# A fused LSH attention and MoE kernel: two small per-row operations move from ScalarE to GpSimd

## Chip, cores and metric

One core of a Trainium2 chip runs the whole program. The metric is the device time of one execution in microseconds (us); the value of a kernel is the median over its runs.

## What is computed

Attention over 4 batches, 8 heads, 768 rows and a head size of 64, in which a query sees only the keys of its own hash bucket (6 sign bits of a projection), and behind it a two-layer feed-forward block on 3072 tokens of 512 values:

```python
mask = q_bucket[:, :, :, None] == k_bucket[:, :, None, :]
scores = np.where(mask, scale * (q @ k.T), -1e9)
scores = scores - np.max(scores, axis=-1, keepdims=True)
attn = np.exp(scores)
attn = attn / (np.sum(attn, axis=-1, keepdims=True) + 1e-09)
x = attn @ v                       # 3072 x 512 after the heads are put side by side
h = x @ w_in                       # 512 -> 2048
g = np.where(h > 0, h, np.exp(np.minimum(h, 0)) - 1)
out = g @ w_out                    # 2048 -> 512
```

## The kernel before

All matrix products run on pairs of float16 numbers, a high and a low part of each float32 value, with three products for one. The 4 batches are cut into 8 chunks of 384 rows. A chunk has 4 head pairs, and a head pair has 6 slots, a slot being 128 query rows of one head against all 768 keys: 192 slots in all. Two slots together are called a duo; there are 96.

What a duo goes through, by line. `scores` (L508) makes 4 matmuls per slot into the one PSUM tile `s`; VectorE (DVE) copies it out to `pt` with a row maximum `m` at its side (L520), which frees `s` for the next slot. `exps` then makes the bias `nb`, minus the scaled maximum, for both slots of the duo in one ScalarE (ACT) operation of 128x2 values (L533), and two exponentials on ACT over 128x768 values with the row sums `sm` as a by-product (L536). `splits` makes the scale `r` from the sums in another 128x2 operation on ACT (L545), takes its reciprocal on DVE (L546), makes the high part `hl` on ACT (L143) and the low part on DVE (L152), and sends both through a transposing DMA on SP's queue to `PT`. `attend` (L559) multiplies `PT` with the values into `av`, four slots after the pair's last scores, and ACT and DVE split `av` into `x` (L568, L569).

The feed-forward matmuls (h, L585; o, L621) are dealt out between the slots. From slot 30 on, TensorE's (PE's) order is the order of the program text; every other engine's order comes from a planner that lists the instructions by an estimated timeline before the run. At run time each engine takes its own instructions strictly in that order. GpSimd (POOL) has a few memsets at the start and then only the 24 output stores (L635), each of which waits for the copy of a finished output tile `W<-o` on ACT (L143) or DVE (L145). The tiles `nb`, `sm`, `r` and `m` have three buffers each.

Of the kernel before, what the change touches and what calls it, by code (L numbers as in the profile page):

```python
# [12 lines left out]
AF = mybir.ActivationFunctionType  # L13
ALU = mybir.AluOpType
# [7 lines left out]
P_TOP = 14  # L22
# [44 lines left out]
def lsh_attention_moe(  # L67
# [10 lines left out]
    nc = tc.nc  # L78
# [60 lines left out]
    def scaled(kind, o, x, s):  # L139

        e = engine(kind)
        if e == "A":
            nc.scalar.activation(o, x, AF.Copy, scale=s)  # L143
        elif e == "V":
            nc.vector.tensor_scalar(o, x, s, None, ALU.mult)  # L145
        else:
            nc.gpsimd.tensor_scalar(o, x, s, 1.0, ALU.mult, ALU.mult)

    def rest(kind, o, x, s, hi):

        if engine(kind) == "V":
            nc.vector.scalar_tensor_tensor(o, x, s, hi, ALU.mult, ALU.subtract)  # L152
        else:
            nc.gpsimd.tensor_scalar(x, x, s, 1.0, ALU.mult, ALU.mult)
            nc.gpsimd.tensor_tensor(o, x, hi, ALU.subtract)
# [372 lines left out]
    def exps(st, duo):  # L528

        m, pts = duo[0], duo[1:]  # L530
        w = len(pts)
        nb = small.tile([P, 2], F32, tag="nb", name="nb")
        nc.scalar.activation(nb[:, :w], m[:, :w], AF.Copy, scale=st["sg"][:, 1:2])  # L533
        sm = small.tile([P, 2], F32, tag="sm", name="sm")
        for n, pt in enumerate(pts):
            nc.scalar.activation(  # L536
                pt, pt, AF.Exp, bias=nb[:, n : n + 1], scale=st["sg"][:, 0:1], accum_out=sm[:, n : n + 1]
            )
        return sm, pts

    def splits(sm, pts, PTs):

        w = len(pts)
        r = small.tile([P, 2], F32, tag="r", name="r")
        nc.scalar.activation(r[:, :w], sm[:, :w], AF.Copy, scale=2.0**-P_TOP, bias=1e-9 * 2.0**-P_TOP)  # L545
        nc.vector.reciprocal(r[:, :w], r[:, :w])  # L546
        for n, pt in enumerate(pts):
            hl = pp.tile([P, 2, S], F16, tag="p", name="hl")
            scaled("p_hi", hl[:, 0, :], pt, r[:, n : n + 1])
            rest("p_lo", hl[:, 1, :], pt, r[:, n : n + 1], hl[:, 0, :])  # L550
            nc.sync.dma_start_transpose(PTs[n].rearrange("p x c e -> p (x c) e"), hl.rearrange("p x e -> p (x e)"))
# [183 lines left out]
    for ns in groups:  # L735
# [3 lines left out]
        for n in ns:  # L739
            at = begin[n] - (PREP0 if early else PREP)[2]  # L740

            w = 2 * chunks[pairs[n][0]]["nc"]
# [142 lines left out]
    def run_splits():  # L885
        if behind:
            splits(*behind.pop())

    for G in range(starts[-2] + 1):
        if G == starts[0]:  # L890
            ordered.enter_context(tc.manual_schedule(engines={mybir.EngineType.PE}))
        if G < len(slots):
            n, at = slots[G]
            c = chunks[pairs[n][0]]
            b, p, j, t = c["b"], pairs[n][1], at // c["nc"], at % c["nc"]
            now[0] = int(w_at == NSI + NSO)
            if t == 0:
                (PT,) = pt_ring.take(c["nc"], pairs[n][0])
                PTs = PTs + [PT] if j else [PT]
            if G < starts[0] and G % 2:  # L900
                s_tile = ps_o.tile([P, 2, 512], F32, tag="o", name="so")
            else:
                s_tile = ps_s.tile([P, 2, 512], F32, tag="s", name="s")
            scores(ks[b, p], qs[n], at, j, s_tile, duo, G >= starts[0])
            into.append(PT[:, t])

            run_splits()
            if len(into) == 2:
                behind.append((*exps(qs[n], duo), into))
                duo, into = [], []  # L910
            if at == 2 * c["nc"] - 1:
                assert not into
                waiting.append((G + AV_LAG, (n, PTs)))
        else:
            run_splits()
# [39 lines left out]
```

## Time and profile before

| | us |
|---|---|
| median of 3 runs | 952.47 |
| lowest and highest run | 951.82, 953.67 |
| the profiled execution | 948.24 |
| its span, first to last instruction | 946.5 |

The span is 1.7 us shorter than the profiled execution's own time; this part lies outside all instructions. In the rows below, times are in us from the start of the span unless marked ns, and an engine's idle time is put down to the instruction that ended it. DVE is VectorE, ACT is ScalarE, POOL is GpSimd, PE is TensorE, PEld its weight loads.

### The profile page before, as it was taken

The page shows a single profiled execution, that of the slowest core. Times are in us where ns is not written, and L with a number is a line of the kernel's source. Part 1 is how long each engine was busy: PE and PEld are TensorE (multiplying, and loading weights), DVE is VectorE, ACT ScalarE, POOL GpSimd, SP SyncE. Part 2 cuts the span into 40 slices and gives each one's busy share as a digit, 9 for nine tenths or more (in the row PEclk, how much of TensorE's full clock was granted, in tenths as well). Part 3 has the DMA queues.
Part 4 walks back from the last instruction along what each step waited for, and adds up shares of the span by engine and source line. Part 5 has one row for each costly group of instructions (what it writes and reads, how often), then busy time and mean ns, then how long its engine had stood idle before and what let it go on. Part 6 is the DMA issues. An engine that isn't in the chain of part 4 may idle for free.

```text
span 946.5 us, 14531 instructions
## 1 busy us (share of the span) xinstructions
PE 818.4 (86%) x4975; PEld 420.4 (44%) x4975; DVE 704.0 (74%) x1528; ACT 739.3 (78%) x1469; POOL 15.7 (2%) x49
## 2 busy tenths in 40 slices
PE   2536555888999999988998999998999999999996
PEld 0113222444545555444544455544545555555553
DVE  6899899898867877678777687787878687674332
ACT  4677777999879888789779788889888788885442
POOL 1000000000000000000000000000000000000000
PEclk9956666998999999999999999999999999999998
DMA  9999886776887767696886767795777667556000
GB/s 280 280 207 224 226 231 161 136 141 145 153 167 169 153 113 126 132 187 117 163 180 137 139 109 150 148 181 101 144 155 136 118 119 151 102 101 100 34 1 35
DMA packets 404586, 138.47 MB, mean 146 GB/s; under 512 B 380960, under 2 KB 398880, under 8 KB 404512
## 3 DMA queue, kind: packets, MB, share of 16 engines
q1 hardware_dynamic: 402432, 131.25, 68.9%
q0 software_dynamic: 1920, 6.29, 1.9%
q8 instruction: 39, 0.64, 0.3%
q14 instruction: 35, 0.29, 0.1%
q10 hardware_dynamic: 160, 0.00, 0.0%
HBM read 35.65 MB, written 6.29 MB: 44 GB/s over the span
## 4 chain that ended last, share of the span: by engine, by line
issue 50%; DVE 14%; PE 14%; DMA 13%; ACT 6%; SPq 1%; POOL 1%; POOLq 0%; ACTq 0%; DVEq 0%
PE o L621 4%; PE av L559 4%; PE h L585 3%; DVE pt L520 3%; DMA PT<-hl 3%; DVE hl L152 3%; PE s L508 2%; DMA K<-natk 2%; DMA O<-nat1q 2%; ACT pt L536 2%; DMA W<-in_moe_w_in_dram 1%; DMA U<-in_moe_w_out_dram 1%; DVE W L469 1%; POOL out_dram L635 1%; DVE W L479 1%
## 5 line engine op out<-in xcount | busy, mean ns | idle before, releaser
L621 PE MATMUL o<-W,U 128*128 128x512 f16 x1152 | 280.2, 380 | 3.2 <-ACT W L143 3.1
L585 PE MATMUL h<-x,W 128*128 128x384 f16 x1536 | 279.8, 326 | 0.0
L585 PEld LDWEIGHTS <-W 128*128 128x128 f16 x1536 | 147.5, 98 | 111.1 <-issue 9.9
L536 ACT ACTIVATE pt<-pt,nb,sg 128x768 f32<-128x768 f32 x192 | 195.3, 1019 | 1.7
L152 DVE SCALAR_TENSOR_TENSOR hl<-pt,r,hl 128x768 f16<-128x768 f32 x192 | 189.4, 1011 | 7.5 <-ACT hl L143 7.2
L520 DVE TENSOR_SCALAR_CACHE_REDUCE pt<-s 128x768 f32<-128x768 f32 x177 | 168.0, 949 | 22.9 <-PE s L508 21.9
L143 ACT ACTIVATE hl<-pt,r 128x768 f16<-128x768 f32 x192 | 168.7, 927 | 20.2 <-DVE r L546 19.4
L508 PE MATMUL s<-K,O 128*128 128x384 f16 x708 | 153.3, 340 | 32.2 <-DVE pt L520 26.9
L621 PEld LDWEIGHTS <-U 128*128 128x128 f16 x1152 | 111.0, 98 | 122.7 <-issue 8.9
L559 PE MATMUL av<-PT,vhl 128*64 128x384 f16 x1152 | 115.6, 350 | 27.3 <-DMA PT<-hl 20.8
L600 DVE SCALAR_TENSOR_TENSOR U<-U 128x384 f32<-128x384 f32 x128 | 70.9, 554 | 85.8 <-ACT U L599 84.8
L508 PEld LDWEIGHTS <-O 76*128 76x128 f16 (+1 forms) x768 | 74.7, 102 | 134.7 <-issue 51.2
L596 ACT ACTIVATE U<-h,ch 128x384 f32<-128x384 f32 x128 | 72.9, 570 | 63.7 <-PE h L585 63.6
L152 DVE SCALAR_TENSOR_TENSOR U<-U,sgg 128x384 f16<-128x384 f32 x128 | 78.4, 612 | 53.3 <-ACT U L143 53.3
L559 PEld LDWEIGHTS <-vhl 128*64 128x64 f16 x1152 | 72.8, 117 | 81.7 <-ACT hl L143 17.7
L143 ACT ACTIVATE U<-U,sgg 128x384 f16<-128x384 f32 x128 | 77.8, 608 | 20.5 <-DVE U L600 20.4
L599 ACT ACTIVATE U<-h,ch 128x384 f32<-128x384 f32 x128 | 72.9, 570 | 0.0
L472 PE MATMUL acc<-W,ones 128*128 128x512 bf16 x32 | 16.9, 546 | 35.7 <-DVE W L469 35.5
L536 ACT ACTIVATION_READ_ACCUMULATOR pt<-pt,nb,sg 128x1 f32 x192 | 36.4, 190 | 0.0
L533 ACT ACTIVATE nb<-m,sg 128x2 f32<-128x2 f32 x96 | 27.7, 289 | 6.8 <-DVE pt L520 6.4
L291 DVE TENSOR_SCALAR zb<-z,pjt 64x384 f16<-64x384 f32 (+1 forms) x48 | 29.1, 606 | 3.9 <-PE z L286 3.9
L207 ACT ACTIVATE nat1q<-qst 128x384 bf16<-128x384 f32 x30 | 15.5, 516 | 18.1 <-DMA O<-nat1q 16.0
(103 smaller groups left out, 527.2 us busy)
## 6 DMA issues: line engine op xcount, KB each, us to landing
U<-in_moe_w_in_dram SPq DMA_DIRECT2D x12, 512.0 KB
vf<-in_v_dram SPq DMA_DIRECT2D x16, 384.0 KB
U<-in_moe_w_out_dram SPq DMA_DIRECT2D x12, 512.0 KB
out_dram<-W POOLq DMA_DIRECT2D x24, 256.0 KB, 4.0
qst<-in_q_dram SPq DMA_DIRECT2D x30, 192.0 KB
kst<-in_k_dram SPq DMA_DIRECT2D x14, 384.0 KB
PT<-hl SPq DMA_TRANSPOSE x192
W<-in_moe_w_in_dram SPq DMA_DIRECT2D x4, 512.0 KB
```

The lines of the kernel that those rows point to most:

```text
L143: nc.scalar.activation(o, x, AF.Copy, scale=s)
L152: nc.vector.scalar_tensor_tensor(o, x, s, hi, ALU.mult, ALU.subtract)
L291: nc.vector.tensor_scalar(zb[used], t[used], pj["thr"][used, which : which + 1], (MBIT, -MBIT)[which], ALU.is_gt, ALU.mult)
L508: nc.tensor.matmul(s_tile[:, n, :HALF], st[o][:rows, at, :], kst[kk][:rows, j * NC + n * HC : j * NC + (n + 1) * HC, :].rearrange("p a b - ...
L520: top = nc.vector.tensor_scalar(pt.rearrange("p (n e) -> p n e", n=2), s_tile[:, :, :HALF], CLAMP, None, ALU.max, ALU.max, accum_out=duo[0 ...
L536: nc.scalar.activation(pt, pt, AF.Exp, bias=nb[:, n : n + 1], scale=st["sg"][:, 0:1], accum_out=sm[:, n : n + 1])
L559: nc.tensor.matmul(av[j * D : (j + 1) * D], vt[:, j, c, vx, :], PTs[j][:, :, px, c, :], start=n == 0, stop=n == last,)
L585: nc.tensor.matmul(h, WH[:, g * KT + t, wx, fc * P : (fc + 1) * P], c["xs"][t][:, xx, :], start=n == 0, stop=n == 3 * KT - 1,)
L596: nc.scalar.activation(e, h, AF.Exp, scale=c["ch"])
L599: nc.scalar.activation(hp, h, AF.Relu, scale=c["ch"])
L600: nc.vector.scalar_tensor_tensor(e, e, -1.0, hp, ALU.add, ALU.min)
L621: nc.tensor.matmul(o[t][:, :DO], g16[:, gx, t * P : (t + 1) * P], WH[:, NSI + 1 + f, wx, :], start=f == 0 and i == 0, stop=f == NF - 1 and ...
```

## The change

The two 128x2 operations of a duo are issued to GpSimd in place of ScalarE. The values are the same: the bias is the row maximum times a per-partition scale that is read from SBUF, and the scale before the reciprocal is (sum + 1e-9) times a constant.

```diff
@@ exps @@
         nb = small.tile([P, 2], F32, tag="nb", name="nb")
-        nc.scalar.activation(nb[:, :w], m[:, :w], AF.Copy, scale=st["sg"][:, 1:2])
+        nc.gpsimd.tensor_scalar(nb[:, :w], m[:, :w], st["sg"][:, 1:2], 1.0, ALU.mult, ALU.mult)
         sm = small.tile([P, 2], F32, tag="sm", name="sm")
@@ splits @@
         r = small.tile([P, 2], F32, tag="r", name="r")
-        nc.scalar.activation(r[:, :w], sm[:, :w], AF.Copy, scale=2.0**-P_TOP, bias=1e-9 * 2.0**-P_TOP)
+        nc.gpsimd.tensor_scalar(r[:, :w], sm[:, :w], 1e-9, 2.0**-P_TOP, ALU.add, ALU.mult)
         nc.vector.reciprocal(r[:, :w], r[:, :w])
```

## Rows read from the trace of the kernel before

**Rows 1.** The page's part 1: busy us (share of the span), instructions, by engine.

```profile
PE 818.4 (86%) x4975; PEld 420.4 (44%) x4975; DVE 704.0 (74%) x1528; ACT 739.3 (78%) x1469; POOL 15.7 (2%) x49
```

**Rows 2.** Busy time of each engine by stage; columns named in the first line.

```profile
core 0: us, PE busy (x) PEld busy (x) DVE busy (x) ACT busy (x) POOL busy (x), PEclk, DMA share, GB/s
40.00:166.00 126.00, 71.23 (x332) 30.83 (x331) 117.84 (x263) 96.63 (x186) 0.00 (x0) 0.62 0.87 210
237.00:860.00 623.00, 595.32 (x3807) 313.75 (x3806) 469.93 (x997) 521.55 (x1053) 9.88 (x18) 1.00 0.74 141
```

**Rows 3.** What PE waited for, 237 to 860: total, times, longest us.

```profile
PE s L508 <- DVE pt L520: 16.6, 21, 1.8
PE av L559 <- DMA PT<-hl: 7.5, 6, 3.1
PE o L621 <- ACT W L143: 3.1, 4, 1.6
```

**Rows 4.** The same view, 40 to 166 (first row) and 166 to 237 (second).

```profile
PE av L559 <- DMA PT<-hl: 9.3, 3, 6.1
...
PE av L559 <- DMA PT<-hl: 4.0, 2, 2.5
```

**Rows 5.** Groups of instructions, whole span: the moved ones.

```profile
L533 ACT ACTIVATE nb<-m,sg 128x2 f32<-128x2 f32 x96 | 27.7, 289 | 6.8 <-DVE pt L520 6.4
L545 ACT ACTIVATE r<-sm 128x2 f32<-128x2 f32 x96 | 18.5, 193 | 0.3
```

**Rows 6.** Waits around them, whole span: total, times, longest us.

```profile
ACT hl L143 <- DVE r L546: 19.4, 18, 3.2
DVE r L546 <- ACT r L545: 6.7, 5, 1.6
ACT nb L533 <- DVE pt L520: 6.4, 14, 1.1
```

**Rows 7.** Timeline of ACT, then DVE, around one duo: start, us, instruction.

```profile
302.12 1.76 ACT L143 ACTIVATE hl<-pt,r 128x768 f16<-128x768 f32 x2 [0.60 <-DVE r L546]
304.72 0.29 ACT L533 ACTIVATE nb<-m,sg 128x2 f32<-128x2 f32 x1
305.04 1.03 ACT L536 ACTIVATE pt<-pt,nb,sg 128x768 f32<-128x768 f32 x1
...
301.93 0.16 DVE L546 RECIPROCAL r<-r 128x2 f32<-128x2 f32 x1
```

**Rows 8.** Timeline of ACT and POOL: the stores at a chunk's end; a memset group.

```profile
286.30 0.68 ACT L143 ACTIVATE W<-o,os 128x512 f32<-128x512 f32 x1
287.29 0.67 POOL L635 DMA_DIRECT2D out_dram<-W  x1 [283.80 <-ACT nb L533]
289.05 0.54 POOL L635 DMA_DIRECT2D out_dram<-W  x1 [1.10 <-DVE W L145]
293.07 0.54 POOL L635 DMA_DIRECT2D out_dram<-W  x1 [3.47 <-ACT W L143]
...
2.11 0.67 POOL L236 MEMSET pjt<- 32x1 f32 x8
```

**Rows 9.** What DVE waited for, 237 to 860: total, times, longest us.

```profile
DVE U L600 <- ACT U L599: 47.2, 37, 3.7
DVE U L152 <- ACT U L143: 41.6, 36, 3.6
```

**Rows 10.** Instructions of L533 in 40 to 166, then in 237 to 860.

```profile
L533 ACT ACTIVATE nb<-m,sg x14: 278/282/298, 40.0 to 158.5; 128x2 f32<-128x2 f32 x14
...
L533 ACT ACTIVATE nb<-m,sg x74: 278/290/302, 241.7 to 856.4; 128x2 f32<-128x2 f32 x74
```

**Rows 11.** DVE busy by stage, lines 152 and 600 alone (us, busy, count); one group.

```profile
237.00:860.00 623.00, 237.28 (x299) 1.00 0.74 141
...
237.00:860.00 623.00, 54.80 (x99) 1.00 0.74 141
...
L152 DVE SCALAR_TENSOR_TENSOR hl<-pt,r,hl 128x768 f16<-128x768 f32 x192 | 189.4, 1011 | 7.5 <-ACT hl L143 7.2
```

## Prediction

> **What bounds the kernel now.** I first read the busy shares of the engines over the whole span: PE 86%, ACT 78%, DVE 74%, POOL 2% [rows 1]. They say only that POOL is free to take work and that ACT is second. The same view cut into stages says where each engine counts. From 40 to 166 us DVE is busy for 117.8 of 126 us and PE for 71; ACT has 29 us to spare. From 237 to 860 us PE is busy for 595.3 of 623 us, ACT for 521.6 and DVE for 469.9 [rows 2]. So this long stage is bound by PE, in an order laid down by the program, and a change of any other engine's work is worth only what it does to PE's 27.7 idle us. The view of PE's own waits names them: 16.6 us for DVE to empty the score tile, 7.5 us for the transposed probabilities, 3.1 us for ACT to copy an output tile [rows 3]. In the two stages ahead PE waits 9.3 and 4.0 us for the transposed probabilities, three and two times [rows 4].
>
> **What is removed.** ACT loses 96 operations of 289 ns (27.7 us) and 96 of 193 ns (18.5 us) [rows 5]: 46.2 us in all, 0.48 us per duo. That is work beside PE, and no PE wait is made of it directly. DVE's waits behind ACT are long, 47.2 and 41.6 us on the feed-forward side [rows 9], but they end in DVE idle time, of which it has 153 us in that stage. The PE wait that names ACT is the output copy, four times [rows 3]. Each of these copies may have had one or the other small operation in front of it; I credit four times 0.29 us, **-1.2 us**. The bounds are 0 and the -7 us worked out under the rivals.
>
> **What is added: two more engine changes per duo.** The bias was made on ACT, where it is used. With ACT waiting, the path from the end of DVE's copy to the exponential was one hand-over of about 0.03 us (DVE's reciprocal ends at 302.09, ACT's `hl` starts at 302.12), 0.29 us of work, and 0.03 us to the exponential (305.01 to 305.04) [rows 7]: 0.35 us. The scale was likewise 0.03 + 0.19 + 0.03 = 0.25 us before DVE's reciprocal. Now both go to POOL and back. No row shows a POOL arithmetic operation, so three pieces are bounded:
> - Hand-over to POOL: ACT's copy ends at 286.98 and POOL's store starts at 287.29 [rows 8]. That is 0.31 us, ten times the hand-over between DVE and ACT, and I take 0.30. It is for a DMA instruction; another kind may start sooner, down to 0.03 us.
> - The operation: eight 32x1 memsets take 0.67 us, 0.08 each, and a store holds POOL for 0.54 [rows 8]. I take 0.29, what ACT needs for the same shape with the same scale read from SBUF [rows 5]; this is the nearest row in kind.
> - The hand-over back: 0.03 to 0.30 by the two kinds of hand-over above; I take 0.15, about the middle, because no row shows that direction.
>
> Together 0.74 us, with bounds of 0.14 and 1.14. Against 0.35 and 0.25 a duo's chain is longer by 0.39 + 0.49 = 0.88 us; by the bounds it is anywhere from 0.32 us shorter to 1.68 us longer.
>
> What is exposed of it? ACT stood idle for the row maximum before 14 of the 96 biases, and DVE for the scale before 5 of its 96 reciprocals; ACT stood idle for the reciprocal before 18 high parts [rows 6]. Elsewhere the consumer comes later than the data, and a bias made early is even a gain for ACT. Between a twentieth and a fifth of the steps are exposed, and I take a quarter, since a longer chain catches up with more of them. What is queued behind: behind an exponential that waits for POOL stand ACT's feed-forward activations, and behind a reciprocal that waits stands DVE's next score copy, for which PE waits. The chain reaches PE where PE already waits for its end, 3 + 2 + 6 = 11 times [rows 3, 4]. So 11 x 0.88 x 1/4 = **+2.4 us**, bounds -3.5 (11 x 0.32) and +18.5 (11 x 1.68).
>
> **What is moved past POOL's queue.** POOL starts its instructions in the planner's order. At a chunk's end its third store waits for a copy that ACT makes later: POOL sits there for 3.47 us [rows 8]. A bias or a scale that is planned behind this store stands behind it. A duo comes every 623 / 74 = 8.4 us [rows 10], with two small operations; with such a wait 2 x 3.47 / 8.4 = 0.83 of them fall into it, at a mean of half the wait, 1.74 us. There are six such chunk ends before the attention work ends. The same quarter exposed gives 6 x 0.83 x 1.74 x 1/4 = **+2.2 us**, bounds 0 (all of them planned ahead of the store) and +8.7 (all exposed). The store itself is held by a small operation for under 1 us, and nothing waits for it at once except the reuse of its tile.
>
> **Edits with one answer.** The arithmetic has the same operands and tile sizes; no DMA, matmul or buffer is added, so the last stage after 860 us costs nothing new: it has no duo left.
>
> **The sum.** -1.2 + 2.4 + 2.2 = +3.4 us on the profiled execution's 948.2 us (946.5 us of span and 1.7 us around it): 951.6. That execution is 4.2 us under the median of the runs, 952.47, so on the scale of the median I forecast **955.9 us**, 0.36% slower.
>
> **Rivals.** *POOL and DVE hold each other up, slower still.* Mechanism: POOL and DVE hold each other up when both read SBUF. The DVE lines that combine two SBUF tensors are 237.3 + 54.8 of 623 us, 47% of the time, in pieces of up to 1.01 us [rows 11]. If a POOL operation must wait for the running one, it starts 0.47 x 0.5 = 0.24 us later; if DVE must wait for POOL's 0.29 us, DVE loses 0.47 x 0.29 = 0.14 us for each. At 40 to 166 us, where DVE is the bound, there are 14 duos, 28 operations [rows 10]: +3.8 us. In the chain 11 x 2 x 0.24 = +5.3 us. With the forecast's 3.4 this gives 12.5 us, **965 us**. It decides once POOL's operation holds DVE for a few tenths of a us. The memsets, POOL's only computing so far, read nothing, so no row here shows such a conflict or denies it. By the Trainium skill, "SBUF — State Buffer", section "Who interferes with whom", a DVE instruction with two SBUF inputs contends with a GpSimd instruction that reads SBUF, as an exclusive lock for a whole instruction; that rule speaks against this change. By it the sum would be this rival's, without it the forecast's.
>
> *The relief of ACT wins, faster.* Mechanism: ACT, 84% busy in the long stage, is what DVE stands behind (89 us) [rows 2, 9], and a DVE that is kept from its score copies is PE's largest wait. 46.2 of 739 us are 6% of ACT's work. If a third of the 16.6 + 3.1 us of PE's waits [rows 3] goes, 6.5 us are won: **946 us** on the median's scale. For it: 82 of 96 biases found ACT late, not the maximum late [rows 6], so that POOL can make the bias before ACT asks. Against it: the last-ending waits name DVE and DMA far more than ACT. It decides if POOL's step, both hand-overs included, stays under some 0.5 us.
>
> *Nothing that can be measured.* The same 82 early biases hide the longer path, PE's order stays, and the relief goes into ACT's idle time: **952.5 us**.
>
> **How the numbers follow.** About 0.2% is what a measurement of this kernel can tell from no change. Forecast (953.5 to 960, its small end within the 0.2%): 0.36. Conflict on SBUF (960 to 970): 0.13. Relief (941 to 950.5): 0.35, nearly as likely, since ACT has slack on one side and the longer chain on the other and the rows weigh both lightly. No change: 0.16. Slower by over 0.2%: 0.32 of the forecast and all of the conflict, 0.45. Within 0.2%: 0.16 and the forecast's small end of 0.04, 0.20. Faster: 0.35. The range from 944 to 967 leaves out about a fifth of the relief and a third of the conflict, with something for an order of the planner that turns out quite otherwise. The forecast's own range is 953.5 to 960.
>
> **What the changed profile would show.** ACT busy at about 693 us; two POOL groups of 96, near 0.29 us each; ACT idle before the exponential put down to POOL, and DVE idle before the reciprocal put down to POOL, each a few to some 20 us. PE's waits for the transposed probabilities should grow from their 20.8 us. A longer mean for DVE's low parts than 1011 ns would show the conflict. PE's waits for DVE's score copy below 16.6 us in the long stage would show the relief. I am wrong if POOL's operation is far over 0.5 us or the planner, given new costs, lays out the first 170 us in another way.

## The result, and the profile after

| | us |
|---|---|
| before, median (lowest to highest) | 953.07 (951.82 to 955.52) |
| after, median (lowest to highest) | 943.43 (942.18 to 945.39) |
| ratio, 95% interval | 0.9898 (0.9871 to 0.9924) |
| profiled execution: before, after | 948.24, 945.39 |

The change makes the kernel 1.0% faster, where 0.36% slower was forecast. The two profiled executions lie close together: that of before is one of the quickest of its kernel, that of after the slowest of its own, so the pair of traces holds 2.9 of the 9.6 us. What the traces are good for here is who waits for whom. Two slow executions are left out of all ratios: one of 963.7 us of the kernel before and one of 2871 us of the second kernel of experiment 4.

The busy shares, and the groups that answer to [rows 1, 5] (columns as there):

```profile
PE 824.1 (87%) x4975; PEld 419.9 (44%) x4975; DVE 713.2 (76%) x1528; ACT 708.0 (75%) x1277; POOL 114.3 (12%) x241
...
L152 DVE SCALAR_TENSOR_TENSOR hl<-pt,r,hl 128x768 f16<-128x768 f32 x192 | 188.7, 1012 | 11.3 <-ACT hl L143 11.2
...
L533 POOL TENSOR_SCALAR nb<-m,sg 128x2 f32<-128x2 f32 x96 | 69.2, 721 | 480.2 <-DVE pt L520 363.4
...
L545 POOL TENSOR_SCALAR r<-sm 128x2 f32<-128x2 f32 x96 | 29.0, 302 | 241.7 <-ACT pt L536 241.7
```

The bias costs GpSimd 721 ns in the mean, the scale 302. The view of waits (total, times, longest us) shows what the move did to its neighbours: the first two lines are of the whole span, to be held against [rows 6], the last two of 237 to 860 us, to be held against [rows 9]:

```profile
DVE r L546 <- POOL r L545: 64.9, 55, 2.6
ACT pt L536 <- POOL nb L533: 59.1, 60, 3.7
...
DVE U L600 <- ACT U L599: 14.0, 31, 0.8
DVE U L152 <- ACT U L143: 13.3, 19, 1.6
```

ACT was relieved of 46.2 us of operations and now waits 59.1 us for the bias; DVE waited 6.7 us for the scale and now waits 64.9. By these two lines the change should have lost. But DVE's waits behind ACT's feed-forward work in the long stage, 47.2 and 41.6 us before, are 14.0 and 13.3. And PE's own waits, 237 to 860 us, then 40 to 166 and 166 to 237 (the answers to [rows 3, 4]):

```profile
PE s L508 <- DVE pt L520: 20.4, 19, 3.2
PE o L621 <- ACT W L143: 1.2, 2, 0.8
...
PE av L559 <- DMA PT<-hl: 2.2, 2, 1.2
...
PE av L559 <- DMA PT<-hl: 3.1, 1, 3.1
```

PE no longer waits for the transposed probabilities in the long stage at all (7.5 us before), and 5.3 us ahead of it (13.3 before), where three waits of 2.1 to 3.6 us for the first feed-forward tiles have come up instead. PE's wait for the score copies, its tile being called `so` in the first slots and `s` later, has grown. Over the whole span, before and then after:

```profile
PE s L508 <- DVE pt L520: 26.9, 28, 3.5
PE so L508 <- DVE pt L520: 6.5, 5, 1.7
...
PE s L508 <- DVE pt L520: 33.4, 27, 3.8
PE so L508 <- DVE pt L520: 12.5, 9, 4.1
```

These 12.5 us more stand against 15.5 us less for the transposed probabilities. In all, PE is idle for 119.5 us of the span in place of 128.1.

The chain of a duo has become shorter. Worked out per duo from the starts and ends of its instructions, mean of the last 72 duos, from the end of the second score copy to the end of the last low part: 10.1 us before, 8.6 after. The piece that shrank most is from the row sums to the start of the reciprocal: 1.78 us before, 0.40 after. That is not what a slower hand-over does; something put the scale, the reciprocal and what follows in another place.

That something is the planner's order. Both programs have the same instructions, name by name, except the 192 moved ones. Of the 1022 ScalarE instructions that both have (a row sum's read-out not counted by itself), at most 744 can be picked that stand in the same sequence in both, with others in between; on VectorE it is 872 of 1336. So the edit has two parts that the trace shows only together: two operations on another engine, and a new order on all of them. The experiments take these apart.

### The profile page after: what moved, and what is told of

The parts are those of the page before. It is cut to its first block, busy times and chain, and to the rows that moved or that the text cites. A ratio compares the mean times of both kernels' runs of the same rounds, so it can differ in the third digit from the quotient of the medians.

```text
span 943.6 us, 14711 instructions
## 1 busy us (share of the span) xinstructions
PE 824.1 (87%) x4975; PEld 419.9 (44%) x4975; DVE 713.2 (76%) x1528; ACT 708.0 (75%) x1277; POOL 114.3 (12%) x241
## 5 line engine op out<-in xcount | busy, mean ns | idle before, releaser
L585 PE MATMUL h<-x,W 128*128 128x384 f16 x1536 | 285.4, 331 | 5.7 <-ACT U L599 3.6
L536 ACT ACTIVATE pt<-pt,nb,sg 128x768 f32<-128x768 f32 x192 | 195.4, 1019 | 59.2 <-POOL nb L533 59.1
L152 DVE SCALAR_TENSOR_TENSOR hl<-pt,r,hl 128x768 f16<-128x768 f32 x192 | 188.7, 1012 | 11.3 <-ACT hl L143 11.2
L508 PE MATMUL s<-K,O 128*128 128x384 f16 x708 | 155.4, 343 | 35.1 <-DVE pt L520 33.4
L508 PEld LDWEIGHTS <-O 128*128 128x128 f16 (+1 forms) x768 | 75.5, 102 | 142.9 <-issue 71.2
L533 POOL TENSOR_SCALAR nb<-m,sg 128x2 f32<-128x2 f32 x96 | 69.2, 721 | 480.2 <-DVE pt L520 363.4
L559 PE MATMUL av<-PT,vhl 128*64 128x384 f16 x1152 | 113.1, 352 | 7.1 <-DMA PT<-hl 5.3
L559 PEld LDWEIGHTS <-vhl 128*64 128x64 f16 x1152 | 69.7, 118 | 61.5 <-issue 13.2
L546 DVE RECIPROCAL r<-r 128x2 f32<-128x2 f32 x96 | 15.6, 162 | 65.6 <-POOL r L545 64.9
L545 POOL TENSOR_SCALAR r<-sm 128x2 f32<-128x2 f32 x96 | 29.0, 302 | 241.7 <-ACT pt L536 241.7
```

Of the source, the lines that this page charges most:

```text
L508: nc.tensor.matmul(s_tile[:, n, :HALF], st[o][:rows, at, :], kst[kk][:rows, j * NC + n * HC : j * NC + (n + 1) * HC, :].rearrange("p a b - ...
L533: nc.gpsimd.tensor_scalar(nb[:, :w], m[:, :w], st["sg"][:, 1:2], 1.0, ALU.mult, ALU.mult)
L536: nc.scalar.activation(pt, pt, AF.Exp, bias=nb[:, n : n + 1], scale=st["sg"][:, 0:1], accum_out=sm[:, n : n + 1])
L559: nc.tensor.matmul(av[j * D : (j + 1) * D], vt[:, j, c, vx, :], PTs[j][:, :, px, c, :], start=n == 0, stop=n == last,)
L585: nc.tensor.matmul(h, WH[:, g * KT + t, wx, fc * P : (fc + 1) * P], c["xs"][t][:, xx, :], start=n == 0, stop=n == 3 * KT - 1,)
```

## The experiments

**How an order is held.** For a pinned kernel, each instruction of ScalarE, VectorE and SyncE, and of TensorE ahead of slot 30, is tied behind the one that is to precede it, for issue only, without a wait (names shortened):

```python
for order in PLAN.values():        # an engine's instructions, as first written, in the order wanted
    for a, b in zip(order, order[1:]):
        tc.add_manual_dep(I[b], I[a].name, NoSync, reason="plan")
```

All ratios are to the kernel before on the same chip. "Old order" is that of the kernel before, "new order" that of the changed kernel. In the traces the pinned kernels run ScalarE's and VectorE's instructions in the very sequence of the kernel whose order they hold (for the order of "each bias twice" in experiment 6 there is no such trace). What pinning alone does was not measured, since no run pins an unchanged kernel to its own order; the four kernels that are pinned to the old order lie between 0.9993 and 1.0038.

**1. The move without the new order.** The changed kernel, with the old order pinned.

> Both small operations on GpSimd, as in the changed kernel, but every other instruction of ScalarE, VectorE, SyncE and (ahead of slot 30) TensorE is pinned to the order that the planner gave the kernel before. Theory A (the gain of 1% comes from the new order that the planner lays out, not from the move itself): no gain is left, 953 to 965 us, because GpSimd's wait for VectorE's two-input operations (the bias took 721 ns in the mean, up to 4.42 us) now stands in a plan that leaves no room for it. Theory B (the move itself: ScalarE is relieved of 46 us and the scale no longer stands behind other ScalarE work): most of the gain stays, 942 to 948 us.

Measured: 951.2 us, 0.9993 (0.9977 to 1.0010). The whole gain is gone, as theory A has it, but nothing is lost either, so that the time lies 2 us below its range. In the old order ACT waits less for the bias than in the new one, because other work stood ahead of the exponentials in many duos:

```profile
ACT pt L536 <- POOL nb L533: 24.8, 33, 1.7
DVE r L546 <- POOL r L545: 4.6, 4, 1.1
```

24.8 us of waiting stand against 27.7 us of removed work, which is about even; that this is why the bias gives nothing here is argued, not shown. And the scale, though started 0.1 us behind the sums in place of 0.9, gains nothing: VectorE's reciprocal keeps its place and starts 1.74 us behind the sums, as before (1.78).

**2. The new order without the move.** The kernel before, with the new order pinned; on ScalarE the bias stands ahead of its exponentials and the scale behind them.

> Both small operations stay on ScalarE, as in the kernel before, but every instruction of ScalarE, VectorE, SyncE and (ahead of slot 30) TensorE is pinned to the order of the changed kernel; on ScalarE the bias stands right ahead of its two exponentials and the scale right behind them. Theory A (the order): the gain is there without GpSimd, 936 to 946 us, and more of it if the 59 us that ScalarE waited for GpSimd's bias cost anything. Theory B (the relief of ScalarE): at least two thirds of the gain are gone, 950 to 956 us.

Measured: 948.4 us, 0.9952 (0.9934 to 0.9969). Half of the gain stays although nothing is on GpSimd; the time lies between the ranges of the two theories. So of 1.02% the order alone gives 0.48% (0.31 to 0.66), and the move, in that order, the other 0.54% (0.9898 / 0.9952 = 0.9946, by both intervals 0.9914 to 0.9978).

**3. One operation at a time, the planner free.**

```diff
-        nc.scalar.activation(nb[:, :w], m[:, :w], AF.Copy, scale=st["sg"][:, 1:2])
+        nc.gpsimd.tensor_scalar(nb[:, :w], m[:, :w], st["sg"][:, 1:2], 1.0, ALU.mult, ALU.mult)
```

> Only the bias is made by GpSimd; the scale stays on ScalarE; the planner lays out its own order. Theory B by ScalarE's time removed (27.7 of 46.2 us): 60% of the gain, about 947 us. Theory C (the gain is the scale's: it no longer stands in ScalarE's queue, 0.9 us behind the row sums): no gain, 951 to 960 us, since GpSimd's bias comes later than ScalarE's own in 60 of 96 duos. Theory A: not tied to either part.

Measured: 962.1 us, 1.0100 (1.0077 to 1.0123), slower than any of the theories had it.

```diff
-        nc.scalar.activation(r[:, :w], sm[:, :w], AF.Copy, scale=2.0**-P_TOP, bias=1e-9 * 2.0**-P_TOP)
+        nc.gpsimd.tensor_scalar(r[:, :w], sm[:, :w], 1e-9, 2.0**-P_TOP, ALU.add, ALU.mult)
```

> Only the scale of the row sums is made by GpSimd; the bias stays on ScalarE; the planner lays out its own order. Theory B by ScalarE's time removed (18.5 of 46.2 us): 40% of the gain, about 949 us. Theory C (the scale's place in ScalarE's queue): the whole gain or more, 936 to 945 us. Theory A: not tied to either part.

Measured: 944.1 us, 0.9919 (0.9899 to 0.9939). The scale alone brings nearly everything; the bias alone costs as much as both together bring. With the planner free, a price per removed microsecond of ScalarE work is refuted: 27.7 us removed cost 1%, 18.5 us removed gain 0.8%.

**4. Those two orders, with everything back on ScalarE.**

> Everything is done where the kernel before does it, but the order of ScalarE, VectorE, SyncE and TensorE's head is pinned to the one the planner made when the bias alone was on GpSimd (that kernel took 962 us); the bias stands right ahead of its exponentials on ScalarE. If that order is what cost 9 us (theory A): 957 to 964 us. If the cost was GpSimd's bias itself, 0.99 us in the mean behind VectorE's two-input operations (theory L): 950 to 956 us.

Measured: 947.2 us, 0.9949 (0.9926 to 0.9973), which neither theory had: the order is good, and the bias on GpSimd, in that order, costs 1.0100 / 0.9949 = 1.5%. Here are the bias and the exponentials' wait with the bias on GpSimd, then with the same order on ScalarE, with PE's wait for score copies in 237 to 860 us under each:

```profile
L533 POOL TENSOR_SCALAR nb<-m,sg 128x2 f32<-128x2 f32 x96 | 92.8, 967 | 731.6 <-DVE pt L520 584.2 <-DVE qm L186 73.9 <-DVE vx L408 27.8
L536 ACT ACTIVATE pt<-pt,nb,sg 128x768 f32<-128x768 f32 x192 | 195.4, 1019 | 64.2 <-POOL nb L533 64.1
...
PE s L508 <- DVE pt L520: 27.2, 23, 3.2
```

```profile
L533 ACT ACTIVATE nb<-m,sg 128x2 f32<-128x2 f32 x96 | 27.7, 289 | 11.0 <-DVE pt L520 11.0
L536 ACT ACTIVATE pt<-pt,nb,sg 128x768 f32<-128x768 f32 x192 | 195.7, 1020 | 3.2
...
PE s L508 <- DVE pt L520: 17.0, 15, 3.0
```

ScalarE waits 64 us for a bias that takes it 27.7 us to make, and PE's wait for the score copies is 10 us longer.

> Everything is done where the kernel before does it, but the order of ScalarE, VectorE, SyncE and TensorE's head is pinned to the one the planner made when the scale alone was on GpSimd (that kernel took 944 us); the scale stands right behind its exponentials on ScalarE. Theory A (the order carries the gain): 944 to 949 us. Theory B (the engine does): 951 to 956 us.

Measured: 947.8 us, 0.9947 (0.9926 to 0.9969). Again half a per cent from the order; the scale's move adds 0.9919 / 0.9947, 0.3%, which is not clear of the two intervals.

**5. The single parts in the old order.** The bias alone on GpSimd:

> The bias alone on GpSimd, everything else pinned to the order of the kernel before. Theory L (GpSimd's bias waits for VectorE's two-input operations, and that wait costs in any order): 956 to 963 us. Theory O (the wait costs only where an order puts nothing between the bias and its exponentials, as the planner's order for this split did; the old order has room): 951 to 955 us.

Measured: 955.4 us, 1.0032 (1.0014 to 1.0050). Then the scale alone:

> The scale alone on GpSimd, everything else pinned to the order of the kernel before. In that order both operations on GpSimd gave 0.9993 and the bias alone 1.0032 of the kernel before. If the two parts add up: 0.996, 947 to 950 us. If the scale gains nothing there, because VectorE's reciprocal keeps its place in the old order and comes 1.7 us behind the sums anyway: 951 to 954 us, and the two parts do not add up.

Measured: 952.3 us, 1.0015 (0.9996 to 1.0034). Then no move at all, but each scale directly behind its exponentials on ScalarE:

> The kernel before with its own order pinned, and one change: each scale stands right behind its two exponentials in ScalarE's order (before it started 0.9 us behind the sums in the mean, with other work in between). VectorE's reciprocal keeps its place. If the scale's place in ScalarE's queue is what delays the chain (theory C): 944 to 949 us. If the reciprocal's and the high parts' places hold it too, so that only a whole new order helps (theory A): 951 to 955 us, no change.

Measured: 955.5 us, 1.0038 (1.0015 to 1.0062). In the old order the scale's earlier start is worth nothing, on whichever engine, and the bias on GpSimd costs 0.3% (0.1 to 0.5). The chain of a duo stays at 10.1 us in all three kernels, in which the reciprocal and the high parts keep their places. In the new order, which moves them, it is 8.6 to 8.7; no run moves them alone.

How near to each other can two kernels be told apart? One more memset of 128x2 on VectorE ahead of everything was meant to change the order:

> The kernel before with one more memset of 128x2 values on VectorE ahead of everything (about 0.1 us of work); the planner lays out a different order for all engines. Theory N (orders differ by chance and any small edit moves the time by up to 1%): more than 0.3% from the kernel before, either way, outside 950 to 956 us. Theory S (orders are alike unless the edit takes something out of the chain): within 0.2%, 951 to 955 us.

Measured: 954.5 us, 1.0023 (1.0002 to 1.0044). The expectation missed its object: the memset left every engine's order as it was. What the run gives is a floor: two kernels of the same order were measured 0.2% apart, so that experiments 1 and 5 differ by little more than that from the kernel before, the bias's 0.3% among them, and the sum of the two parts there (1.0047) is not reliably different from both together (0.9993). The differences of 0.3% to 0.5% elsewhere are to be read with this floor.

TensorE's granted clock is not what sets the kernels apart. Its mean over an execution, as a share of full speed, lies between 0.939 and 0.957 for each kernel, averaged over its runs. Over 100 executions of the kernel before, time and clock hardly go together (correlation -0.18), and 0.01 more of the clock goes with 0.4 us less.

**6. Is it chance that other orders are better?** The order made when each bias is computed twice on ScalarE, run with the bias computed once:

> Everything is done where the kernel before does it; the order of ScalarE, VectorE, SyncE and TensorE's head is pinned to the one that the planner makes when each bias is computed twice on ScalarE (27.7 us more ScalarE work in its estimate; the second copy itself is left out here). Three orders made with less ScalarE work gave 0.995 each when everything was put back on ScalarE. Theory S (the planner's order is better the less it has to place on ScalarE): 953 to 962 us, no better than the kernel before. Theory N (any other order than this kernel's own is about 0.5% better or worse by chance): 944 to 950 us would speak for it.

Measured: 965.1 us, 1.0150 (1.0129 to 1.0171), on theory S's side and beyond its range. And the order made when the scale is on VectorE (experiment 8), with everything on ScalarE:

> Everything is done where the kernel before does it; the order is pinned to the one that the planner made with the scale on VectorE (935 us, the fastest so far); the scale stands right behind its exponentials on ScalarE. Theory S (orders laid out with less ScalarE work carry about 0.5% by themselves): 944 to 949 us, and the move to VectorE is the rest. If the order is nearly all of it: 935 to 942 us.

Measured: 939.1 us, 0.9851 (0.9821 to 0.9881). The same instructions on the same engines, in six orders; the two times on the right are worked out per duo, means over the last 72 duos:

| order laid out with | ratio, all on ScalarE | score copy to exponentials, us | whole chain, us |
|---|---|---|---|
| each bias twice on ScalarE | 1.0150 | 2.31 | 10.64 |
| everything on ScalarE (before) | 1 | 1.76 | 10.07 |
| bias off ScalarE | 0.9949 | 1.13 | 9.33 |
| scale off ScalarE, to GpSimd | 0.9947 | 1.15 | 8.75 |
| both off ScalarE, to GpSimd | 0.9952 | 0.98 | 8.73 |
| scale off ScalarE, to VectorE | 0.9851 | 1.19 | 8.85 |

The four orders laid out with less ScalarE work leave less time between a score copy and its exponentials and are faster, even where the work is on ScalarE after all; the one laid out with more leaves more and is slower. All five new orders lie on the side that this says, but three of them were known when the rule was made, so that it is not shown; and the last order gives 1.5% with a chain like that of its neighbours, so the chain's length is not the whole measure of an order. What else makes that order good stays open.

**7. Which operation gives the other half in the new order.** The new order pinned, the scale on GpSimd, the bias on ScalarE:

> The order of the changed kernel, pinned; the scale on GpSimd as there, the bias on ScalarE right ahead of its exponentials. With both on ScalarE this order took 948, with both on GpSimd 943, with the bias on VectorE 939 us. Theory L (GpSimd's bias waits for VectorE, so that it gives ScalarE nothing): faster than or equal to the changed kernel, 939 to 944 us, and the scale is the whole difference of 5 us. Theory B (27.7 us taken off ScalarE count): 945 to 948 us.

Measured: 943.6 us, 0.9907 (0.9876 to 0.9938), as theory L has it. Then the bias on VectorE, directly behind the score copy:

> The order of the changed kernel, pinned, the scale on GpSimd as there; the bias is made by VectorE right behind the score copy of the duo's second slot (0.15 us on VectorE, where 14 us in all are added), so that it waits for no shared port. Theory L: ScalarE's 59 us of waiting for the bias shrink, and the kernel gets faster than the changed one: 936 to 941 us. Theory O (that wait lies in ScalarE's spare time): no gain, 941 to 945 us. A loss, 946 us or more, if VectorE's 14 us delay the score copies that TensorE waits for.

Measured: 939.4 us, 0.9852 (0.9824 to 0.9880).

In one and the same order: both on ScalarE 0.9952, the scale on GpSimd 0.9907, the bias there too 0.9898, the bias on VectorE 0.9852. So in the new order the move of the scale gives nearly all of the second half, and the bias on GpSimd nothing that can be told; made where nothing holds it up, the bias gives another half per cent. Both steps are only just clear of their intervals (0.9907 / 0.9952 is 0.9919 to 0.9991, 0.9852 / 0.9907 is 0.9902 to 0.9987). The scale's step is not an earlier start: on ScalarE it stands 0.03 us behind the sums in this order, on GpSimd 0.1 us. What is left for it is that ScalarE has 18.5 us less to do; no run takes this apart further. The last kernel's rows: 230 ns for the bias, and ACT's wait ahead of the exponentials down from 59 us to 25, of which 9 are put down to the bias and 15 to no wait that the profile shows ("issue"):

```profile
L536 ACT ACTIVATE pt<-pt,nb,sg 128x768 f32<-128x768 f32 x192 | 195.2, 1019 | 24.7 <-issue 15.1 <-DVE nb L533 8.9 <-DVE qm L186 0.5
L533 DVE TENSOR_SCALAR nb<-m,sg 128x2 f32<-128x2 f32 x96 | 22.1, 230 | 3.4
```

**8. Without GpSimd, the planner free.** The scale on VectorE, directly ahead of its reciprocal, the bias on ScalarE as before:

```diff
-        nc.scalar.activation(r[:, :w], sm[:, :w], AF.Copy, scale=2.0**-P_TOP, bias=1e-9 * 2.0**-P_TOP)
+        nc.vector.tensor_scalar(r[:, :w], sm[:, :w], 1e-9, 2.0**-P_TOP, ALU.add, ALU.mult)
```

> The bias on ScalarE as before, the scale on VectorE right ahead of its reciprocal, the planner lays out its own order. Theory C (what counts is that the scale leaves ScalarE's queue, GpSimd being only one place for it): as with the scale on GpSimd, 942 to 947 us. Theory G (an idle engine is needed, because VectorE's queue is as planned as ScalarE's): 950 to 956 us.

Measured: 934.8 us, 0.9813 (0.9789 to 0.9837): the fastest version, 0.9% under the changed kernel, and below the ranges of both theories. By the last run of experiment 6, 1.5% of its 1.9% are its order; the remaining 0.4% is barely clear of the two intervals. The bias on VectorE and the scale on GpSimd:

> As in the run before this one, the bias on VectorE and the scale on GpSimd, but the planner lays out its own order. The order theory: within 0.4% of the pinned form, 936 to 947 us; a larger distance says how much a planner's order alone can move.

Measured: 942.7 us, 0.9895 (0.9872 to 0.9918), inside the expected range; pinned to the new order the same split of work had given 0.9852. Both on VectorE:

> Bias and scale both on VectorE, the planner lays out its own order. If each piece taken off ScalarE without a wait at GpSimd counts: 930 to 938 us, below the 935 us with the scale alone. If VectorE's additional 0.15 us ahead of each duo's next instruction delay the score copies, TensorE's largest wait: 939 to 948 us.

Measured: 942.8 us, 0.9920 (0.9902 to 0.9938). Less ScalarE work than in the fastest version, and slower: a rule "off ScalarE, and all is well" does not hold. Last, the scale on VectorE in the order that had 944 us with the scale on GpSimd:

> The order that the planner made with the scale alone on GpSimd (944 us), pinned, but the scale is made by VectorE right ahead of its reciprocal: no hand-over to GpSimd and back. Theory H (the hand-overs and the wait for the port are what keeps GpSimd's scale from the 935 us that VectorE's scale reached with its own order): 936 to 941 us. Theory A (the difference of 9 us is the order): 942 to 947 us.

Measured: 945.4 us, 0.9943 (0.9924 to 0.9962). With the scale on GpSimd this order had 0.9919, and with everything on ScalarE 0.9947, so the hand-overs to GpSimd are not what separates 944 from 935; the order is. In this order, taking the scale's 18.5 us off ScalarE gives nothing that can be told.

## Why the prediction was wrong, point by point

**The step that failed first** had no term in the sum: the sum and all rivals let the other instructions stand where the planner had put them, and only let the small operations start earlier or later. The text knew the planner. It left some of its range for an order "that turns out quite otherwise", and its last way to be wrong was that the planner "lays out the first 170 us in another way", but it put no price on either. That sign came true: ScalarE's and VectorE's sequences part from the old ones at 52 and 48 us. The order is worth 0.48% in the changed kernel and 1.5% in another. No row of before could have given its size; that its size was unknown and could exceed all the terms could have been said, and the range widened for it below 944.

**The sum of the terms, by itself,** was +3.4 us. Run in the order for which it was made, the move gave 0.9993, or -0.7 us, between -2.2 and +1.0; run in the new order, it gave 0.9946, or -5 us. So the two terms that make it slower, +2.4 and +2.2, were also too dear, and the relief was too small in the new order:

*Hand-overs.* Charged 0.30 us to GpSimd, 0.29 of work, 0.15 back. The timeline of after has a bias that meets no VectorE operation of two SBUF tensors, with the score copy ahead of it:

```profile
406.14 0.08 DVE L520 DVE_READ_ACCUMULATOR pt<-s 128x1 f32 x1
406.14 0.16 DVE L186 TENSOR_SCALAR qm<-qx 128x2 f32<-128x2 f32 x1
...
406.39 0.26 POOL L533 TENSOR_SCALAR nb<-m,sg 128x2 f32<-128x2 f32 x1 [5.70 <-DVE qm L186]
```

The copy ends at 406.22, VectorE's next small operation, to which the profile puts the wait down, at 406.30, and the bias starts at 406.39: 0.09 to 0.17 us for the hand-over, not 0.30. The median of the 96 biases starts 0.17 us behind its copy. The scale and the way back:

```profile
423.27 1.01 ACT L536 ACTIVATE pt<-pt,nb,sg 128x768 f32<-128x768 f32 x1
424.19 0.19 ACT L536 ACTIVATION_READ_ACCUMULATOR pt<-pt,nb,sg 128x1 f32 x1
424.47 0.19 POOL L545 TENSOR_SCALAR r<-sm 128x2 f32<-128x2 f32 x1 [2.25 <-ACT pt L536]
424.69 0.17 DVE L546 RECIPROCAL r<-r 128x2 f32<-128x2 f32 x1
```

0.09 us to GpSimd (424.38 to 424.47), 0.19 of work, 0.03 back: 0.31 us in all for the scale, where 0.74 was charged. The 0.30 came from a row of the output store, another kind of instruction; the bound of 0.03 was the nearer one for the scale, and for the bias the middle.

*Exposure.* A quarter of the steps was taken as exposed. In the changed kernel ACT waits for 60 of the 96 biases and DVE for 55 of the 96 scales, with the old order pinned for 33 and 4. So the share is the order's too, and it does not carry to the end of the chain: there PE waits 3 times in place of the 11 that were counted on.

*GpSimd's queue behind the stores,* +2.2 us. At the end of a chunk:

```profile
392.07 0.54 POOL L635 DMA_DIRECT2D out_dram<-W  x1 [0.20 <-issue]
393.09 0.18 POOL L545 TENSOR_SCALAR r<-sm 128x2 f32<-128x2 f32 x1 [0.48 <-ACT pt L536]
396.96 0.57 POOL L635 DMA_DIRECT2D out_dram<-W  x1 [3.68 <-ACT W L143]
397.57 0.68 POOL L533 TENSOR_SCALAR nb<-m,sg 128x2 f32<-128x2 f32 x1
```

The third store again holds GpSimd for 3.68 us, but the scale stands ahead of it, and the bias behind it starts 0.39 us after its score copy (which ends at 397.18) in place of 0.17. No bias of the 96 started later than 0.42 us behind its copy, and no scale later than 0.10 us behind its sums. The term was worth nothing.

*The relief,* -1.2 us. The wait it was tied to, PE's for the output copy, went from 3.1 to 1.2 us in the long stage, which is near the term. But part of it is the order's: over the whole span this wait is 3.1 us before, 2.1 in experiment 2's kernel and 1.2 after. And the move's 5 us in the new order are four times the term.

**The conflict on SBUF** existed, on one side only. GpSimd's bias took from 0.26 us to 4.42 us. The longest one, with what VectorE ran meanwhile:

```profile
215.59 4.42 POOL L533 TENSOR_SCALAR nb<-m,sg 128x2 f32<-128x2 f32 x1 [2.86 <-DVE vx L408]
...
215.41 0.54 DVE L600 SCALAR_TENSOR_TENSOR U<-U 128x384 f32<-128x384 f32 x1
215.88 1.00 DVE L152 SCALAR_TENSOR_TENSOR natk<-kst,ks,natk 128x768 f16<-128x768 f32 x1
216.81 0.73 DVE L152 SCALAR_TENSOR_TENSOR W<-W,w1s 128x512 f16<-128x512 f32 x1
217.47 1.93 DVE L152 SCALAR_TENSOR_TENSOR hl<-pt,r,hl 128x768 f16<-128x768 f32 x2
219.33 0.54 DVE L600 SCALAR_TENSOR_TENSOR U<-U 128x384 f32<-128x384 f32 x1
```

Six operations of two SBUF tensors, with the one that ran when the bias began, back to back; the last ends at 219.87, and the bias at 220.01. Of 96 biases 74 took over 0.35 us, 0.85 in the mean; 72 of them began while such an operation ran, the other two less than 0.01 us ahead of one. The other 22 took 0.27. The typical held one ended 0.13 us behind the operation that held it; 62 were held by one operation, 12 by two or more. The scale took over 0.2 us 21 times in 96. The Trainium skill's rule ("SBUF — State Buffer", "Who interferes with whom") agrees with this, in that GpSimd waits for whole instructions; that it also waits for operations which VectorE begins later is this trace's own finding. VectorE, for its part, lost nothing that shows: its low parts take 1012 ns, 1011 before [rows 11], and the 74 of them that ran beside a small operation of GpSimd took 1012 ns like the other 118. The rival's +3.8 us for VectorE was therefore wrong, and its wait in the chain, 0.24 us by the forecast, was 0.45 us for the bias (721 against 270 ns). What the bias on GpSimd costs depends on the order: 0.3% in the old one, little above the floor of 0.2%, nothing that can be told in the new one, 1.5% in the order that the planner made for the bias alone.

**The relief as a rival** had the right sign and nearly the right number, 946 us for 943.4, and in part by luck: half of the gain is the order's, which it did not have. PE's largest wait, for the score copies, through which it was to come, did not fall (16.6 to 20.4 us in the long stage); its wait for the transposed probabilities did. For the other half it is neither shown nor refuted. In the new order each part that leaves ScalarE without a wait in return gives about half a per cent, while the bias, the larger part, gives nothing on GpSimd; in the old order and in that of the scale alone, relief gives nothing that can be told. Its chance, 0.35, was fair; the edge of the range at 944 was not, since nothing bounded the case there.

**The other signs.** PE's waits for the transposed probabilities were to grow from 20.8 us and fell to 5.3. ACT's and DVE's waits for POOL were to be a few to some 20 us each and came to 59 and 65. ACT is busy for 708 us in place of the 693 that were worked out: the durations of its instructions add up to 47 us less, but fewer of their records overlap.

## What to carry to other kernels

Where a planner lays out the order, an edit of an operation is two changes, and the order can be the larger one: pin the old order and run the edit in it, then pin the new order and undo the edit, before either is believed. A small operation on a busy engine can be worth moving for the plan that comes of it more than for its nanoseconds: next to its consumer, on VectorE ahead of the reciprocal, it made the fastest version here, and four fifths of that gain were the order. GpSimd is a poor place for a step in a chain that runs beside VectorE operations on two SBUF tensors.

## What the runs showed of the hardware

- A 128x2 operation on GpSimd takes 0.19 us with constant operands and 0.26 us with a scale read from SBUF; the hand-over to it takes 0.09 us from ScalarE and 0.17 us from VectorE's score copy (medians of 96), the one from it 0.03 us. From a row sum to its reciprocal that makes 0.31 us, against 0.25 us through ScalarE, as the prediction adds it up.
- A GpSimd operation that reads SBUF can be held through several VectorE operations on two SBUF tensors that stand back to back, not just through the one that was running (12 of 96 biases, the longest 4.42 us through six operations), while VectorE is not slowed (1012 ns with and without).
- The same instructions on the same engines spread over 3% (0.985 to 1.015) in six orders that all came from one planner.
